# Attention with decay and a mixer on one core: idle matmuls placed by the planner's gaps, a score piece cut in two, wider low-part weights, another order

## The chip, the cores and the metric

The kernel runs on one core of one Trainium2 chip. The time is device time in microseconds (us) of one launch. Before the change it took 1146.36 us, the median of 3 runs (1143.42 to 1152.19). Where the text speaks of engines it uses the names of the profile: PE is the matrix engine, PEld its weight loads, DVE the vector engine, ACT the scalar engine, POOL the GpSimd engine, SP the queue that issues transfers.

## What is computed

All inputs are float32. There are 8 batches of 8 heads, with a sequence of 576 and a head size of 64, so 512 channels. First comes causal attention with a decay, then a mixer over tokens and channels:

```python
log_f = np.log(np.clip(f, 0.0001, 1.0)); cum = np.cumsum(log_f, axis=-1)
scores = scale * (q @ k.T) + cum[:, None] - cum[None, :]      # causal
attn = softmax(scores);  x = attn @ v                         # per head, then heads side by side
xt = x.transpose(0, 2, 1)
h = np.maximum(xt @ w_tok1, 0.0) @ w_tok2                     # 576 -> 256 -> 576
u = x + h.transpose(0, 2, 1)
out = u + np.maximum(u @ w_ch1, 0.0) @ w_ch2                  # 512 -> 1536 -> 512
```

## The kernel before

**Two parts.** The first part, some 690 us of the span, does the attention of all 64 heads, the token mixer, and the channel mixer for the first 256 of its 1536 hidden columns. The second part does the other 1280 hidden columns for nine blocks of 512 tokens: 2160 matmuls of 512 columns each, one behind the other (L819 to L842).

**High and low parts.** To keep float32 accuracy on a faster matmul type, an operand is split into a high part (its value rounded) and a low part (the rest). A product of two split operands is three matmuls: high by high, high by low, low by high.

**A head pair.** Two heads are loaded together (`raw`), q and k are split into `hl`, and their scores are computed by three score steps, `scores` (L504). The head size is 64, so a score matmul uses 64 of the 128 rows of the array; the two heads of a pair lie in the upper and lower half, and both halves work at the same time. A step computes some row blocks of head 0 and others of head 1. The row blocks (`where`, L494) have 64, 192, 320, 448 and 576 score columns; the one of 576 is computed as two pieces of 288. `PLACES` (L502) is the order of the pieces in a step: the first step has 288 and 288 in one half, 448 and 64 in the other; the second has 448 and 64 beside 320 and 192; the third 320 and 192 beside 288 and 288. Each list is gone through four times, for high by high, low by high, high by low, and the decay. A step is thus 16 matmuls (L519), each with a load of its own weights.

**The rest of a head.** DVE takes the masked row minimum (L560), ACT the exponential (L567), POOL divides by the row sum (L593), PE transposes the probabilities (L607), ACT and DVE split them, and PE multiplies them with the values into `av` (L677 to L689). The values lie as `vv`, 128 columns wide: 64 of the high part and 64 of the low part. The high part of the probabilities is multiplied with all 128 columns (L689); their low part with the first 64 alone (L687). ACT and DVE add the two halves of the result into `xt` (L727, L734, L737). The first four heads are done without the split.

**PSUM.** The first pair of banks (`pairs[0]`, kind `sc`) holds the 576-wide score blocks; the second (`pairs[1]`, kind `av`) the sums of `av`; four single banks hold all else (`one`).

**What sets the order.** Nothing is written in the order in which it runs. Each operation is given to a planner, `Plan.op`, with an engine, a duration, a priority and its buffers. `Plan.run` plays the program with these durations: on each engine the ready operation of the lowest priority number is taken next, if its buffers are free. The order in which operations start there is the order of the program, engine by engine; each engine then works through its own list, and waits where an operand isn't ready. The priorities are the table `PR`: one number for each operation of each head or mixer step, found by a search. A score step's duration in the plan is worked out from its columns (`flow`, L521).

**Idle matmuls.** `fill` (L346) gives the planner 120 small matmuls of the identity with itself, into an `av` buffer that nobody reads, with the worst priority there is, from a planned time of 8.5 us on. PE takes one wherever it has nothing else, until the 120 are used up.

Of the kernel before, what the change touches and what calls it, by code (L numbers as in the profile page):

```python
# [15 lines left out]
P = 128  # L16
PRM = dict(
    FILL=120, EP=3, DLAST=1, F1=2, FV=4, n_raw=2, n_vr=2, n_hl=2, n_vv=2,
# [5 lines left out]
    load=(-49.42, 46.29, 92.32, -145.75, 158.83, 224.67, 392.43, 389.92, 51.72, -48.13, -153.64, 61.83, 93.55, 627.95, -379.01, -179, 102.9, 208.23, 313.33, -46.54, 77.82, 682.62, 583.35, 565.73, 618.77, 476.42, 210.51, 132.03, -5.16, 471.13, 807.5, 123.55,),  # L24
    vload=(260.89, -123.21, -87.6, -152.37, -253.12, 178.61, -271.5, 143.23, -99.57, -242.66, 73.14, -320.19, -310.84, 74.82, 236.19, 70.39, -273.25, 388.84, -0.22, -78.47, -129.44, 469.63, 181.63, 387.34, 385.04, 230.17, 266.43, 60.11, 177.61, 138.15, -295.68, -169.11,),
    hi=(-129.17, -415.12, -86.61, 108.68, 306.45, -531.69, -232.24, 165.51, -110.63, -192.03, 59.44, 397.5, 237.73, -147.47, 14.26, -308.52, -51.97, -159.87, 7.58, 219.17, 246.51, -266.63, -191.79, 13.99, 118.63, -34.92, 136.84, 221.46, -3.49, 128.31, 0.66, -310.18,),
    lo=(-489.63, -34.98, 182.79, 104.62, -125.46, -287.97, -331.87, 31.39, 196.89, 23.66, -413.95, -451.42, 205.39, -749.32, -108.87, -107.11, 139.51, 29.45, -369.92, -169.78, -526.87, -68.1, 20.38, -250.48, -344.54, 32.69, 0.4, -425.79, -319.03, -206.8, 30.01, -364.65,),
    vh=(-31.37, -30.76, -94.41, -113.4, -515.02, -327.92, -378.35, -236.94, -123.95, -222.98, -393.91, -204.08, -65.62, -266.02, -57.45, -210.12, -445.93, -449.4, 241.14, -61.99, -170, -302.26, 92.7, -173.08, 59.29, 87.72, -184.46, 12.37, 222.89, 59.12, -54.28, -35.71,),
    vl=(560.64, 122.14, 152, 332.3, 65.87, -132.79, 356.3, -113.35, 230.75, 109.79, -25.3, 263.93, 170.51, 88.24, 216.55, -184.22, 82.02, 171.22, 163.44, 232.62, 254.57, -1.67, 94.46, -138.66, -53.34, -221.02, 284.67, 404.97, -273.49, -10.98, -61.7, -82.46,),
    s1=(125.56, 126.13, 107.5, 181.46, 251.3, -11.07, -68.97, -38.23, 111.08, -55.96, 102.57, 107.08, 620.08, 37.06, 38.4, 53.85, 56.06, -39.81, 90.27, 59.68, -34.99, 41.66, 60.32, 71.83, -4.82, 74.81, -75.81, 125.97, 101.21, 120.47, 95.31, 376.09,),  # L30
    s2=(-19.7, 325.83, -148.1, -274.85, -298.9, -96.51, -258.3, -199.59, 45.51, 1.37, -122.92, -387.8, 99.01, -173.56, -15.5, -267.47, -145.97, -162.18, 57.83, 246.58, 36.34, -417.88, 163.49, -11.16, -132.89, -15.37, -70.87, 132.08, -91.72, -104.46, -252.21, -23.22,),
    s3=(-106.81, -657.17, -171.91, -118.29, -371.64, -432.82, -87.4, -395.44, -313.1, -119.42, -181.81, -20.34, -248.25, -78.96, -171.97, -92.86, -158.9, -377.85, -86.62, -94.1, -200.53, -134.42, -176.82, 32.33, -174.48, -160.27, -110.2, -254.33, -277.72, -259.16, -31.29, -29.24,),
    mn4=(212.64, -151.19, 33.65, -60.63, 54.93, 214.65, 102.81, -42.6, -10.05, 258.69, 464.19, -23.01, 224.98, 253.21, 138.99, 85.09, -231.68, 137.58, 254.41, 84.48, 247.24, 35.75, 45.25, 101.38, -42.51, 181.55, 121.66, -140.73, -15.32, 23.02, 127.35, 86.04, 78.93, -65.2, 8.69, 352.28, 72.2, -73.1, 147.81, 158.41, -2.32, -23.53, -75.47, 58.34, 130.08, 187.04, 132.9, 77.49, 94.23, -51.57, 153.57, 25, -113.13, 30.6, 210.83, 114.09, 180.91, 164.75, 233.74, 327.77, 201.31, 361.67, 108.31, 100.26,),
    ex4=(192.92, 130.59, 156.67, -19.3, -289.51, 161.85, 302.86, -62.62, -65.42, 92.51, -3.84, -41.44, 59.97, -215.72, 87.59, 5.81, 203.67, 134.11, -135.58, 82.91, -215.04, 165.06, 405.95, 196.86, -28.28, 41.97, -65.17, 45.14, -70.21, 90.92, 108.74, -219.16, 255.08, 233.37, 17.69, 170.33, 289.37, 22.54, 199.44, 363.62, -174.81, -28.32, -100.02, -28.94, -283.21, 141.99, 88.75, 26.92, -70.16, 216.53, 107.37, 146.65, 244.62, -97.85, -46.68, 57.2, 202.95, 330.3, -50.94, -185.29, 39.67, 206.02, 374.73, 143.02,),
# [46 lines left out]
class Plan:  # L81
# [14 lines left out]
    def op(self, eng, dur, prio, fn, rd=(), wr=(), bufs=(), lat=0, at=0.0, port=False, span=None):  # L96
# [26 lines left out]
        for d in deps:  # L123
            d.outs.append(o)
        for b in bufs:
            b.left += 1
        self.ops.append(o)
        return o

    def run(self, slots):  # L130

        free = {k: None for k in slots}
        busy_unit = {}
        engines = {}
        for o in self.ops:
            engines.setdefault(o.eng, [])
# [43 lines left out]
        while left:  # L180
            moved = False
            for e, lst in ready.items():
# [71 lines left out]
def build(nc, env, dims):  # L254
# [97 lines left out]

    for i in range(PRM["FILL"]):
        fill(i)
# [862 lines left out]
```

## Time and profile before

| what | us |
|---|---|
| median of 3 runs | 1146.36 |
| lowest, highest | 1143.42, 1152.19 |
| the profiled execution, its time | 1153.54 |
| its span, from the first to the last instruction | 1151.7 |
| mean granted clock of PE | 0.987 |
| busy time in the span: PE, DVE, ACT, POOL | 1106.1, 630.6, 558.8, 526.0 |

The profiled execution took 7.2 us more than the median. A row of the profile names the line, the engine, the operation, the tile it writes and those it reads; "PE busy" counts matmuls from their start to a modelled end, and matmuls are pipelined, so that the distance between two starts says more than one duration. The granted clock is 1.00 at full speed.

### The profile page before, as it was taken

To read this page: it belongs to the slowest core of one execution; us is meant where nothing else is said; L and a number is where in the kernel's file an instruction comes from. 1 tells how busy PE (TensorE), PEld (TensorE's weight loads), DVE (VectorE), ACT (ScalarE), POOL (GpSimd) and SP (SyncE) were. 2 spreads that over 40 slices of the span, in tenths; PEclk is the share of its full clock that TensorE was granted. 3 is DMA by queue.
4 is the path that set the end of the run, shared out by engine and by line. 5 is a ranking of instruction groups with operands and counts; after the bars stand their busy time and mean duration, and the time that the engine had idled before them with its cause. 6 is when DMAs were issued, how large, how long until landed. Compare 5 with 4: busy or idle time off the path is not lost.

```text
span 1151.7 us, 19870 instructions
## 1 busy us (share of the span) xinstructions
PE 1106.1 (96%) x7310; PEld 955.8 (83%) x7310; DVE 630.6 (55%) x1622; ACT 558.8 (49%) x1441; POOL 526.0 (46%) x611
## 2 busy tenths in 40 slices
PE   8987786999999999999999999999999999999998
PEld 7676675998999899889999888888888888888886
DVE  7578787878767787787777996121212121212111
ACT  6577666767777787787786543121111111111110
POOL 2788676783848786786662403220303030312010
PEclk9999898999999999999999999999999999999999
DMA  5232222233212223222103543321203030302010
GB/s 183 64 97 66 81 75 95 95 112 112 86 52 90 103 65 116 86 86 84 35 22 119 199 153 125 101 71 40 83 27 110 1 110 1 110 1 73 18 56 37
DMA packets 47490, 93.20 MB, mean 81 GB/s; under 512 B 6688, under 2 KB 24096, under 8 KB 46368
## 3 DMA queue, kind: packets, MB, share of 16 engines
q1 hardware_dynamic: 47392, 91.93, 24.4%
q8 instruction: 57, 0.93, 0.3%
q14 instruction: 41, 0.34, 0.1%
HBM read 63.60 MB, written 28.31 MB: 80 GB/s over the span
## 4 chain that ended last, share of the span: by engine, by line
PE 85%; DVE 6%; ACT 4%; POOL 2%; issue 2%; DMA 0%; SPq 0%; DVEq 0%; ACTq 0%; POOLq 0%
PE bank L607 8%; PE bank L820 7%; PE bank L819 7%; PE bank L821 7%; PE pair L841 7%; PE pair L840 7%; PE pair L842 7%; PE bank L519 7%; PE pair L689 3%; PE pair L687 3%; PE pair L519 2%; PE pair L677 2%; PE bank L1032 1%; ACT pr L567 1%; PE bank L1004 1%
## 5 line engine op out<-in xcount | busy, mean ns | idle before, releaser
L301 POOL TENSOR_TENSOR ring<-xt,ring 128x512 fp32r<-128x512 f32 (+1 forms) x68 | 93.0, 1384 | 333.6 <-ACT ring L295 332.3
L307 DVE SCALAR_TENSOR_TENSOR hid<-bank,hid 128x512 fp32r<-128x512 f32 x90 | 62.2, 691 | 334.2 <-ACT hid L295 334.2
L295 ACT ACTIVATE hid<-bank 128x512 fp32r<-128x512 f32 x90 | 53.8, 598 | 344.1 <-PE bank L821 343.9
L593 POOL TENSOR_SCALAR pr<-pr,rec 128x576 f32<-128x576 f32 (+4 forms) x320 | 163.5, 532 | 12.2 <-DVE rec L586 7.1
L295 ACT ACTIVATE p<-bank 128x384 fp32r<-128x384 f32 (+2 forms) x300 | 130.8, 475 | 49.1 <-PE bank L607 46.7
L607 PE MATMUL bank<-ident,pr 128*128 128x128 f32 (+1 forms) x960 | 145.7, 285 | 7.4 <-ACT pr L567 2.5
L841 PE MATMUL pair<-hid,w2r 128*128 128x512 f32 x360 | 140.1, 389 | 0.0
L840 PE MATMUL pair<-hid,w2r 128*128 128x512 f32 x360 | 140.1, 389 | 0.0
L820 PE MATMUL bank<-ring,w1r 128*128 128x512 f32 x360 | 140.1, 389 | 0.0
L821 PE MATMUL bank<-ring,w1r 128*128 128x512 f32 x360 | 140.0, 389 | 0.0
L819 PE MATMUL bank<-ring,w1r 128*128 128x512 f32 x360 | 140.0, 389 | 0.0
L842 PE MATMUL pair<-hid,w2r 128*128 128x512 f32 x360 | 140.0, 389 | 0.0
L607 PEld LDWEIGHTS bank<-ident,pr 128*128 128x128 f32 (+1 forms) x960 | 111.0, 136 | 27.7 <-ACT pr L567 4.9
L304 DVE TENSOR_TENSOR p<-bank,p 128x384 fp32r<-128x384 f32 (+1 forms) x180 | 106.1, 595 | 46.4 <-ACT p L295 44.9
L567 ACT ACTIVATE pr<-bank,nmin 128x448 f32<-128x448 f32 (+3 forms) x256 | 117.9, 468 | 23.3 <-DVE nmin L560 21.0
L560 DVE CUSTOM_DVE_ANT_0 bank<-bank,mask 128x320 f32<-128x320 f32 (+3 forms) x256 | 105.9, 442 | 22.8 <-PE bank L519 20.2
L519 PE MATMUL bank<-hl 64*128 64x64 f32 (+3 forms) x768 | 103.7, 308 | 2.9 <-DVE hl L489 1.8
L519 PEld LDWEIGHTS bank<-hl 64*128 64x128 f32 x768 | 83.9, 185 | 12.3 <-issue 3.0
L819 PEld LDWEIGHTS bank<-ring,w1r 128*128 128x128 f32 x360 | 67.6, 188 | 14.1
L842 PEld LDWEIGHTS pair<-hid,w2r 128*128 128x128 f32 x360 | 67.6, 188 | 14.0
L821 PEld LDWEIGHTS bank<-ring,w1r 128*128 128x128 f32 x360 | 67.5, 188 | 14.0
L841 PEld LDWEIGHTS pair<-hid,w2r 128*128 128x128 f32 x360 | 67.6, 188 | 14.0
(123 smaller groups left out, 2611.3 us busy)
## 6 DMA issues: line engine op xcount, KB each, us to landing
raw<-in_qk SPq DMA_DIRECT2D x32, 576.0 KB, 3.7
vr<-in_v SPq DMA_DIRECT2D x32, 320.0 KB, 2.9
ud<-xt SPq DMA_DIRECT2D x8, 1152.0 KB, 4.8
pd<-part SPq DMA_DIRECT2D x32, 288.0 KB, 2.1
out_t<-part SPq DMA_DIRECT2D x36, 256.0 KB, 2.6
d_raw<-in_w_ch SPq DMA_DIRECT2D x12, 512.0 KB, 3.5
d_raw<-in_w_ch SPq DMA_DIRECT2D x40, 128.0 KB, 3.0
xt<-ud SPq DMA_DIRECT2D x2, 1024.0 KB, 5.4
```

The lines of the kernel that those rows point to most:

```text
L295: nc.scalar.activation(out, in_, func, scale=scale)
L304: nc.vector.tensor_tensor(out, in_, asf(hi), op=ALU.subtract)
L519: nc.tensor.matmul(at(bs[x])[:m, of : of + w], left, right, start=first, stop=(z == 3), skip_group_check=True)
L567: nc.scalar.activation(at(pr)[:m, poff[t] : poff[t] + w], at(mybanks[k])[:m, of : of + w], AF.Exp, bias=E["nmin"][sm][:m, t : t + 1], scal ...
L593: nc.gpsimd.tensor_scalar(x, x, r, 0.0, op0=ALU.mult, op1=ALU.add)
L607: nc.tensor.transpose(out, at(pr)[:, poff[i] + start[j] : poff[i] + end[j]], E["ident"])
L819: nc.tensor.matmul(q, wh[:, c, :], h_, start=(c == 0), stop=False)
L820: nc.tensor.matmul(q, wl[:, c, :], h_, start=False, stop=False)
L821: nc.tensor.matmul(q, wh[:, c, :], l_, start=False, stop=(c == NC - 1))
L840: nc.tensor.matmul(q, wh, h_, start=(i == i0), stop=False)
L841: nc.tensor.matmul(q, wl, h_, start=False, stop=False)
L842: nc.tensor.matmul(q, wh, l_, start=False, stop=(i == NF - 1))
```

## The change

Four things are changed.

1. The 120 idle matmuls are no operations of the plan any more. When the plan is done, `run` goes through PE's list: where the planned start of an operation lies more than 400 ns behind the planned end of the one before (from 8.5 us on, and before the first operation of the second part), it puts in one idle matmul for every 112 ns of what is left of the gap after 150 ns. They are the same 64x64 product, but into the first pair of banks. There are 295 of them, in 44 groups: 47 in the first seven groups, 194 in the next 23, up to about the twentieth head, and 54 in the last 14. In 22 groups the first one waits for ACT or DVE: for the last reader of the score block that lies in that pair.
2. The score piece of 448 columns becomes two of 224 (`where`, `PLACES`), in the first two of the three score steps; these have 20 matmuls now. In the plan a step's duration is a constant (`SPANS`).
3. The low part of the probabilities is multiplied with all 128 columns of `vv`, not with 64. (The product of both low parts is thus added too.)
4. The planner adds the weight load ahead of an operation in full, where PE has stood idle, and the table `PR` is another one.

```diff
@@ PRM, PR
-    FILL=120, EP=3, DLAST=1, F1=2, FV=4, n_raw=2, n_vr=2, n_hl=2, n_vv=2,
+    EP=3, DLAST=1, F1=2, FV=4, n_raw=2, n_vr=2, n_hl=2, n_vv=2,
...
-    dec=(261.24, 234.03, -24.46, -117.88, 95.57, 16.32, -323.96, 147.46, 519.87, 667.7, 406.35, 248.6, -223.23, 335.2, 62.47,),
+    dec=(261.34, 336.18, -183.68, -1335.72, 449.89, 121.06, -247.23, 1292.58, -192.72, -183.15, 398.74, 395.04, -323.94, 832.72, 1008.01,),
@@ Plan.run
-    def run(self, slots):
+    def run(self, slots, each=112.0, spare=150.0, least=400.0):
...
-                    o.start += max(0.0, o.head - tail - (t - engine_at[e]))
+                    o.start += o.head if t > engine_at[e] else max(0.0, o.head - tail)
...
-        return order
+        out, at, seen, fit = [], 8500.0, 0.0, True
+        for o in order:
+            if o.eng == "PE":
+                fit = fit and not any(b.kind == "acc" for b in o.bufs)
+                for _ in range(int((o.start - max(at, seen) - spare) / each) if fit and o.start - max(at, seen) > least else 0):
+                    out.append(None)
+                seen = o.start + o.dur
+            out.append(o)
+        return out
@@ build
-    def fill(i):
-        av = Buf("av")
-        p.op(
-            "PE", [tp_(64, 64)] * 2, 1e6 + i, lambda: nc.tensor.matmul(at(av)[:64, :64], E["ident"][:, :64], E["ident"][:, :64], start=True, stop=True),
-            rd=[("fill", i - 1)], wr=[("fill", i)], bufs=[av], at=8500.0,
-        )
-
-    for i in range(PRM["FILL"]):
-        fill(i)
...
-        3: (0, [(0, 0, end[3])]),
+        3: (0, [(0, 0, end[3] // 2), (end[3] // 2, end[3] // 2, end[3] // 2)]),
...
-    PLACES = (((0, 0, 0), (1, 0, 0), (0, 0, 1), (1, 1, 0)), ((0, 0, 0), (1, 0, 0), (1, 1, 0), (0, 1, 0)), ((0, 0, 0), (1, 0, 0), (1, 0, 1), (0, 1, 0)))
+    PLACES = (
+        ((0, 0, 0), (1, 0, 0), (0, 0, 1), (1, 0, 1), (1, 1, 0)),
+        ((0, 0, 0), (1, 0, 0), (0, 0, 1), (1, 1, 0), (0, 1, 0)),
+        ((0, 0, 0), (1, 0, 0), (1, 0, 1), (0, 1, 0)),
+    )
+    SPANS = (1130, 1130, 1160)
...
-                        first = z == 0 and (x, u, s) != (0, 1, 0) and (x, u, s) != (1, 1, 0)
+                        first = z == 0 and u == 0 and (s == 0 or t == 4)
...
-            flow = [sum(where[t][1][s][2] + 30 for x, u, s in places if x == y for t in [units[x][u]]) for y in (0, 1)]
...
-                bufs=[*bs, hl, cc, *prs], span=4 * max(flow) / 2.4,
+                bufs=[*bs, hl, cc, *prs], span=SPANS[st],
...
-                elif z:
-                    nc.tensor.matmul(x[:D], at(vv)[:, v0 + j, :D], at(pb)[:, 1, c0 : c0 + w], start=False, stop=last)
                 else:
-                    nc.tensor.matmul(x, at(vv)[:, v0 + j, :], at(pb)[:, 0, c0 : c0 + w], start=False, stop=last)
+                    nc.tensor.matmul(x, at(vv)[:, v0 + j, :], at(pb)[:, z, c0 : c0 + w], start=False, stop=last)
...
-            return [tp_(w, D)] * 2 if fv else [mm_(w, D if z else P)]
+            return [tp_(w, D)] * 2 if fv else [mm_(w)]
@@ attn_mixer_kernel
-            o.fn()
+            if o is None:
+                nc.tensor.matmul(pairs[0][:64, :64], ident[:, :64], ident[:, :64], start=True, stop=True)
+            else:
+                o.fn()
```

**The idle matmuls, on PE.** The place is the seam between a score step and the product of the next head with its values, some ten heads into the kernel; pair_63 is the first pair of banks, pair_64 the second, hl the split q and k, p the split probabilities, cc and sel the decay. In the kernel before:

```order
L519 MATMUL bank_66<-cc_181,sel 128x448
L519 MATMUL bank_68<-cc_181,sel 128x320
L519 MATMUL bank_68<-cc_181,sel 128x192
L519 MATMUL bank_66<-cc_181,sel 128x64
L677 MATMUL pair_64<-p_179,vv_169 128x512 [waits DVE_49,Pool_49]
L678 MATMUL pair_64<-p_179,vv_169 128x64
```

and in the changed one:

```order
L525 MATMUL bank_65<-cc_181,sel 128x224
L525 MATMUL pair_63<-cc_181,sel 128x288
L525 MATMUL bank_65<-cc_181,sel 128x224
L525 MATMUL bank_65<-cc_181,sel 128x64
L1186 MATMUL pair_63<-ident 64x64 [waits DVE_49]
L1186 MATMUL pair_63<-ident 64x64 x6
L682 MATMUL pair_64<-p_179,vv_169 128x512 [waits Activation_49,Pool_49]
```

Seven idle matmuls now stand between the two; the first waits for DVE, and the product behind it can't start before they are done.

**The score step, on PE.** The place is the first score step of a head pair; the pair of banks takes the pieces of one half of the array, the single bank those of the other. Before, the first round of the list and half of the second:

```order
L519 MATMUL pair_63<-hl_167 128x288
L519 MATMUL bank_68<-hl_167 128x448 [waits DVE_49]
L519 MATMUL pair_63<-hl_167 128x288
L519 MATMUL bank_68<-hl_167 128x64
L519 MATMUL pair_63<-hl_167 128x288
L519 MATMUL bank_68<-hl_167 128x448
```

and now:

```order
L525 MATMUL pair_63<-hl_167 128x288
L525 MATMUL bank_65<-hl_167 128x224 [waits DVE_49]
L525 MATMUL pair_63<-hl_167 128x288
L525 MATMUL bank_65<-hl_167 128x224
L525 MATMUL bank_65<-hl_167 128x64
L525 MATMUL pair_63<-hl_167 128x288
L525 MATMUL bank_65<-hl_167 128x224
```

The half that had two matmuls in a round has three.

**The low-part products, on PE.** The place is the end of a head's product with its values; L607 and L612 are transposes. Before:

```order
L687 MATMUL pair_64<-p_178,vv_169 64x512
L689 MATMUL pair_64<-p_178,vv_169 128x512
L607 MATMUL bank_68<-ident,pr_170 64x128 [waits Activation_49]
L607 MATMUL bank_68<-ident,pr_170 64x128 x3
L687 MATMUL pair_64<-p_177,vv_169 64x384
L689 MATMUL pair_64<-p_177,vv_169 128x384
L607 MATMUL bank_66<-ident,pr_170 128x128 [waits Activation_49]
L607 MATMUL bank_66<-ident,pr_170 128x128 x3
L689 MATMUL pair_64<-p_175,vv_169 128x128
L687 MATMUL pair_64<-p_175,vv_169 64x128
L687 MATMUL pair_64<-p_175,vv_169 64x256
L689 MATMUL pair_64<-p_175,vv_169 128x256
```

and now:

```order
L692 MATMUL pair_64<-p_178,vv_169 128x512 x2
L612 MATMUL bank_68<-ident,pr_170 128x128 x4
L692 MATMUL pair_64<-p_177,vv_169 128x384 x2
L692 MATMUL pair_64<-p_175,vv_169 128x128 x2
L692 MATMUL pair_64<-p_175,vv_169 128x256 x2
L1186 MATMUL pair_63<-ident 64x64 [waits Activation_49]
```

The matmuls with 64 output rows (64 weight columns) have become such of 128.

More of the change, by code (lines that the diff above doesn't have):

```diff
@@ L55 @@
-    dec=(261.24, 234.03, -24.46, -117.88, 95.57, 16.32, -323.96, 147.46, 519.87, 667.7, 406.35, 248.6, -223.23, 335.2, 62.47,),
-    dec3=(255, 25.19, 499.74, 240.41, 567.3, -35.26, 303.23, 374.53, 943.87, 473.14, 15.68, 538.77, 239.12, 427.46, 113.5, 413.03, 54.45, 726.31, -291.68, 188.64,),
+    load=(-26.73, 348.68, -358.7, 122.05, 324.23, -0.33, -122.99, -24.62, 685.99, 667.1, -479.32, 410.03, 81.06, 337.64, 196.53, 75.93, 383.27, 363.51, 785.72, 522.6, 273.36, 765.15, -6.37, 1052.06, 476.09, -84.99, -167.06, -288.69, 379.79, 594.27, -287.98, 943.95,),
@@ new lines @@
+    vload=(845.68, -924.72, -1126.55, -934.92, -352, 355.5, -404.65, -341.25, 303.04, 68.76, -556.5, 477.26, 10.88, 665.03, 279.55, 206.64, 237.9, 379.23, 332.57, -13.11, -752.27, -631.35, -163.64, -127.64, 344.58, -417.03, -191.73, 74.37, 728.52, 427.92, -370.46, -413.02,),
+    hi=(-114.51, -153.5, -196.61, 102.29, -496.82, -102.33, -545.96, -70.78, -459.5, 316.23, -30.58, -212.26, -353.33, -167.74, -656.64, 46.01, 161.55, -73.1, 59.29, -34.72, -506.16, 28.52, 319.79, 357.98, -260.28, -722.21, 406.89, 73.5, -232.67, -306.36, 381.71, -1068.88,),
@@ new lines @@
+    lo=(-310.59, -165.92, 143.75, -613.39, -463.53, -621.67, 344.22, -457.84, 196.98, 23.57, 209.18, 34.15, -37.41, -569.78, 24.91, -209.74, 207.72, 212.77, -122.22, 436.03, -245.07, 186.67, -671.59, -705.05, 375.29, 70.63, 165.6, -755.32, -106.92, -37.55, -23.2, -140.82,),
+    vh=(-129.29, -210.57, -122.35, -207.5, 181.64, -124.39, -100.97, -425.53, -230.48, -683.14, -401.82, -1.06, 239.27, -183.92, -377.6, 205.6, 54.62, 90.64, -280.74, -448.12, 765.03, -316.2, -163.34, -11.69, -85.27, -684.47, -96.37, -62.66, -259.85, 366.19, -246.6, 409.46,),
@@ new lines @@
+    vl=(-167.12, -70.45, 299.09, 122.7, 267.82, 156.47, -333.23, 20.1, 916.32, 558.9, 137.92, -225.84, 595.83, -212.99, -158.6, 462.91, 0.29, -318.43, -335.07, 1261.47, 541.79, -244.27, 672.57, 103.15, 304.68, 107.86, -133.22, -158.2, -377.77, 20.53, -621.72, -663.56,),
+    s1=(-185.93, -55.69, -459.38, -70.2, 430.22, 179.86, -49.96, -641.16, 908.39, 172.58, 801.82, 73.51, -411.44, 232.48, 89.49, 12.42, -267.97, -344.02, 57.95, 64.32, -208.48, 51.72, 183.62, -502.18, 22.81, -4.61, 219.91, 106.66, 79.65, 301.44, 157.94, -51.65,),
@@ new lines @@
+    s2=(-211.54, 111.53, -125.77, -118.05, 73.33, 335.78, 284.27, 277.34, 34.01, -404.44, 13.27, 207.9, 540.14, -626.43, -140.97, -58.83, -284.99, -653.89, 173.47, -584, -22.16, -488.23, -254.24, 418.22, -88.46, -76.01, 50.87, 43.05, -95.76, -175.64, 142.56, -148.81,),
+    s3=(-1315.91, -346.52, 313.26, -117.06, -251.98, -482.32, -283.9, -189.53, -362.78, -743.44, -317.25, -216.57, -468.72, -187.28, -536.36, -449.6, -105.27, -288.64, -324.14, -689.66, -195.22, -347.34, -518.32, -334.72, -250.63, -413.8, 55.74, -255.91, -194.33, 13.98, -389.93, -601.06,),
```

54 lines of the change are left out of this document (23 added, 31 removed).

## The prediction

> **What bounds the kernel now.** I read the page first, then the busy time by stage (the window view, cut where PE changes its habits), then the half-speed windows of PE, then the chain.
>
> ```profile
> span 1151.7 us, 19870 instructions
> PE 1106.1 (96%) x7310; PEld 955.8 (83%) x7310; DVE 630.6 (55%) x1622; ACT 558.8 (49%) x1441; POOL 526.0 (46%) x611
> ...
> 0.00:75.00 75.00, 70.21 (x638) 51.47 (x639) 51.00 (x169) 48.73 (x141) 43.62 (x67) 1.00 0.38 120
> 75.00:200.00 125.00, 95.86 (x736) 82.84 (x735) 96.32 (x272) 83.58 (x236) 91.18 (x113) 0.89 0.23 75
> 200.00:690.00 490.00, 483.49 (x3919) 443.46 (x3919) 390.28 (x1043) 353.87 (x944) 304.47 (x364) 1.00 0.28 95
> 690.00:1152.00 462.00, 456.55 (x2022) 378.06 (x2020) 92.99 (x142) 72.57 (x125) 86.71 (x68) 1.00 0.19 61
> ```
>
> The columns are the busy times of PE, its weight loads, DVE, ACT and POOL, then PE's granted clock, DMA share and GB/s. PE is the bound from 200 us on: 6.5 us idle in 490, and the last stage, which the change leaves alone, is a closed row of matmuls. Between 75 and 200 us nothing is full: PE is idle for 125 - 95.86 = 29.1 us, yet its clock is 0.89. Cut to 3.41 us, that stretch has these windows at half speed, all there are before 1140 us (the first row is a full-speed one):
>
> ```profile
> 126.04:129.45 3.41, 1.80 (x16) 1.49 (x14) 3.39 (x15) 2.66 (x9) 0.12 (x1) 1.00 0.00 0
> 81.66:85.08 3.42, 3.32 (x13) 2.77 (x14) 1.84 (x8) 2.42 (x9) 3.42 (x5) 0.50 0.35 85
> 112.38:115.80 3.42, 3.42 (x16) 2.88 (x15) 2.09 (x6) 2.48 (x9) 3.42 (x5) 0.50 0.27 73
> 119.21:122.62 3.41, 2.90 (x12) 2.53 (x13) 1.10 (x4) 0.84 (x3) 2.00 (x2) 0.50 0.10 14
> 129.45:132.86 3.41, 3.41 (x16) 2.85 (x15) 2.67 (x8) 2.98 (x11) 0.80 (x1) 0.50 0.30 84
> 146.52:149.93 3.41, 3.41 (x17) 3.14 (x16) 2.21 (x5) 2.28 (x7) 1.31 (x2) 0.50 0.00 0
> 173.83:177.24 3.41, 0.65 (x3) 0.58 (x4) 2.55 (x6) 1.18 (x3) 2.40 (x3) 0.50 0.34 70
> 177.24:180.65 3.41, 3.41 (x17) 2.96 (x16) 1.36 (x3) 1.18 (x3) 2.04 (x5) 0.50 0.25 103
> 184.07:187.48 3.41, 3.41 (x14) 2.84 (x15) 1.28 (x4) 1.18 (x3) 1.36 (x2) 0.50 0.32 96
> ```
>
> The window ahead of 129.45 had PE busy 1.80 of 3.41 us, about half, and half speed followed; so it is ahead of the others. When PE then gets its work, it does it at half speed: 16 matmuls fill a window. The chain of waits shows what that does:
>
> ```profile
> 75.20 0.88 PE bank L607 x8
> ...
> 82.58 1.76 PE bank L607 x8
> ...
> 116.08 2.85 POOL pr L593 x6
> ...
> 120.57 1.76 PE bank L607 x8
> ...
> 184.66 1.76 PE bank L607 x8
> ```
>
> The same eight transposes take 0.88 us at full speed and 1.76 at half, and they lie on the chain. At 112 to 119 us POOL is the chain, and at 173.83 PE had next to nothing to do.
>
> **The change part by part.** The sum is made against the profiled execution: 1153.54 us, a span of 1151.7 and 1.8 around it, which is 7.2 above the median of 1146.36.
>
> *Idle matmuls.* Until 75 us the old ones stand and the clock is 1.00 throughout; behind them it falls. The new ones stand in the gaps that follow (194 of them up to about the twentieth head), so the half-speed windows should go. Worth at most half of PE's busy time in the eight: 3.32 + 3.42 + 2.90 + 3.41 + 3.41 + 0.65 + 3.41 + 3.41 = 23.9, half of it 12.0 us. Without the two windows where PE is not the chain it is 19.9, half of it 9.9. DVE, at 96 of 125 us, is late next, so I take -8, between -3 and -12. The idle matmuls themselves lie in idle time, 29.1 us of it. What they add is a wait: PE works in order, and in 22 groups the first one waits until DVE and ACT have read the 576-wide score block; behind it stand transposes and products of other heads, for which in turn ACT and DVE wait. The two reads that may be outstanding:
>
> ```profile
> L560 DVE CUSTOM_DVE_ANT_0 pair<-pair,mask 128x576 f32<-128x576 f32 x64 | 49.9, 779 | 5.9 <-PE bank L519 5.8
> L567 ACT ACTIVATE pr<-pair,nmin 128x576 f32<-128x576 f32 x64 | 47.4, 740 | 28.8 <-DVE nmin L560 27.5 <-PE bank L519 1.2
> ```
>
> So a wait costs from nothing to 0.78 + 0.74 = 1.5 us. Most groups stand in planned gaps of the stretch where PE waits anyway; I take +1 in all, with 22 x 1.5 = 33 as the far end.
>
> *Score halves.* One first step, PE and then its loads:
>
> ```profile
> 420.80 0.29 PE L961 MATMUL bank<-t2h,ring 128*128 128x288 f32 x1
> 421.01 0.40 PE L519 MATMUL pair<-hl 64*128 64x288 f32 x1
> ...
> 421.67 0.44 PE L519 MATMUL bank<-hl 64*128 64x448 f32 x1
> 421.78 0.29 PE L519 MATMUL pair<-hl 64*128 64x288 f32 x1
> 421.91 0.30 PE L519 MATMUL pair<-cc,sel 64*128 64x288 f32 x1
> 421.95 0.19 PE L519 MATMUL bank<-hl 64*128 64x64 f32 x1
> ...
> 422.26 0.19 PE L519 MATMUL bank<-cc,sel 64*128 64x64 f32 x1
> 422.38 0.55 PE L607 MATMUL bank<-ident,pr 128*128 128x128 f32 x3
> ```
>
> ```profile
> 421.33 0.18 PEld L519 LDWEIGHTS bank<-hl 64*128 64x128 f32 x1
> ...
> 421.44 0.19 PEld L519 LDWEIGHTS bank<-hl 64*128 64x128 f32 x1
> ```
>
> The step takes 422.38 - 421.01 = 1.37 us. The half with 288 and 288 goes at 0.13 a piece, 0.26 a round; the half with 448 and 64 needs 422.26 - 421.95 = 0.31 a round and sets the step. Two loads for the same half, one straight after the other, start 0.11 apart. A short matmul can't hide that: the 64-column piece costs a load, 0.11, and 448 columns 0.20. At the pace of the 288 piece 224 columns take 0.13 x 224 / 288 = 0.10, less than a load. So a round becomes three loads, 0.33 us, and a step 4 x 0.02 = 0.08 longer. The same pieces are in the second step. The window view of two lines alone says how many there are in the dense stage:
>
> ```profile
> 200.00:690.00 490.00, 88.64 (x1024) 76.16 (x1024) 1.00 0.28 95
> ...
> 200.00:690.00 490.00, 54.40 (x184) 21.55 (x184) 1.00 0.28 95
> ```
>
> The first row is L519: 1024 / 16 = 64 steps in the stage that PE bounds, two thirds of them changed, 43 x 0.08 = +3.4; with some of the 12 before 200 us, +4. The other end: if loads didn't bind, the 0.26 of the other half would set the round, 43 x 4 x 0.05 = -8.6.
>
> *Low-part products.* The second row above is L687: 184 / 4 = 46 heads there. The end of one such product, and its loads:
>
> ```profile
> 418.89 0.31 PE L689 MATMUL pair<-p,vv 128*128 128x128 f32 x1
> 419.04 0.34 PE L687 MATMUL pair<-p,vv 128*64 128x128 f32 x2
> 419.22 0.28 PE L689 MATMUL pair<-p,vv 128*128 128x256 f32 x1
> 419.34 0.29 PE L959 MATMUL bank<-t2h,ring 128*128 128x288 f32 x1
> ```
>
> ```profile
> 418.98 0.20 PEld L687 LDWEIGHTS pair<-p,vv 128*64 128x64 f32 x2
> 419.10 0.19 PEld L689 LDWEIGHTS pair<-p,vv 128*128 128x128 f32 x1
> ```
>
> Two loads of 64 columns take 0.12 together, 0.06 each, half of the 0.11 above; so the two 128-column matmuls, which are short enough to be bound by the load behind them, take 0.06 each now and 0.11 with 128-column weights: +0.10 a head. The products of 256 to 512 columns hide either load. 46 x 0.10 = +4.6, and +5 with a little of the 13 earlier heads; as much as +7 where the short first product (L678) is followed by such a load, and about 0 if all were hidden.
>
> The Trainium skill says otherwise (TensorEngine Tiling (Array Packing), Key Properties): changing the tiling mode drains TensorE, and 128x64 is another mode than 128x128. By that rule leaving the 64-column form saves drains; that is the fourth rival below. The trace shows a drain where the rows change (above, 420.80 to 421.01, 0.21 instead of the 0.13 of its kind, so 0.08) but none at the columns, where 0.06 is the load alone.
>
> *The new order.* It moves every engine's list and the transfers (the DMA share of 0.23 to 0.28 leaves these room). What it can win is idle PE: 4.8 + 29.1 + 6.5 = 40 us before 690 us. In the dense stage a searched order left 6.5 of 490; the 29 are where there is something to find. I take -8, a quarter of these, between +4 and -25.
>
> Sum: -8 + 1 + 4 + 5 - 8 = -6, so 1147.5 for an execution like the profiled one. Of the 7.2 us by which that one lies above the median I put half down to its half-speed windows, which need not fall alike in each run, and which the forecast has already taken out; the other half comes off: 1144.
>
> **The rivals.** *The order pays more* (faster): half of the 40 us of idle time, 20 rather than 8. For it: the stretch to 200 us is bound by no engine. Against: the same waits on DVE and POOL stand in any order. 1144 - 12 = 1132. (A score round of 0.26 would come to the same, 1144 - 4 - 8.6 = 1131.)
>
> *The idle matmuls block PE* (slower): the waits of the 22 groups for the score block's readers come late in fact, since the planned times aren't the real ones. At 0.7 us each they cost 15 us and push the time over 1% up; at 1 us, 1144 + 21 = 1165. For it: the reads take 1.5 us. Against: 16 of the 22 stand before about 200 us, where PE has 29 us to spare.
>
> *The clock isn't kept* (the change doesn't do what it says): real gaps aren't where the plan has them, half-speed windows remain, 1144 + 8 = 1152. Against: the old ones kept it until 75 us.
>
> *Column modes drain*: six changes a head (two at each of three places) at the 0.08 of the row change, 46 heads, give -22, and the +5 falls away: 1144 - 27 = 1117. Against: the loads above.
>
> **How the numbers follow.** A measurement of this kernel can tell about 1% from no change: below 1134.9 is faster, above 1157.8 slower. The forecast, 1144 within 1%, gets 0.58; the clock not kept, which also ends within 1%, 0.10; the order paying more 0.21; column modes 0.03; blocked PE 0.08. So faster 0.24, same 0.68, slower 0.08. The range goes from 1129, which takes in most of the second case, to 1157; outside it lie the column modes, the blocked PE and a good third of the better order, 0.03 + 0.08 + 0.08.
>
> **What would show it.** Clock: no half-speed windows between 75 and 200 us, and the eight transposes at 0.88 us everywhere. Scores: 1.45 us for the first step, loads of the half with three pieces 0.11 apart. Low parts: in the last group of a head 0.22 us, not 0.12, from the first load of a low part to the load behind the second. Idle matmuls: hardly any wait of theirs for ACT or DVE in the list of waits. Order: PE's idle time before 690 us falls from 40 by about 8, beyond what the clock gives. If PE's idle time grows or the clock stays at 0.89, the prediction is wrong in its first step; if the score step falls below 1.37, in its second.

## The result, and the profile after

| | before | after |
|---|---|---|
| first comparison, medians in us (4 runs each) | 1146.62 | 1159.27 (1157.69 to 1159.59) |
| its ratio, 95% interval | | 1.0102 [1.0062, 1.0143] |
| repeated beside the experiments (19 and 10 runs) | 1151.69 | 1157.77 (1156.94 to 1159.54) |
| its ratio, 95% interval | | 1.0058 [1.0040, 1.0077] |
| the profiled execution, its span | 1153.54, 1151.7 | 1159.12, 1157.3 |

The change makes the kernel slower, by 0.4 to 1.4%; the forecast was 1144, in a range that ends at 1157. The kernel before had medians of 1151.4 to 1151.9 in each of the later sessions, so 1.0058 is the better figure, some 7 us. Prices below are differences of ratios to the runs of before beside them, times 1151.5 us.

First the page of the changed kernel and its busy time by stage (PE, its loads, DVE, ACT, POOL; granted clock, DMA share, GB/s):

```profile
span 1157.3 us, 21062 instructions
PE 1135.2 (98%) x7916; PEld 994.4 (86%) x7916; DVE 622.9 (54%) x1622; ACT 560.8 (48%) x1441; POOL 527.4 (46%) x611
...
PE 94%; DVE 3%; ACT 2%; issue 1%; DMA 0%; SPq 0%; DVEq 0%; ACTq 0%
```

```profile
0.00:75.00 75.00, 68.90 (x583) 51.31 (x584) 52.33 (x176) 49.80 (x142) 44.63 (x68) 0.95 0.38 118
75.00:200.00 125.00, 116.38 (x1155) 104.50 (x1154) 93.40 (x274) 85.28 (x240) 93.39 (x115) 0.97 0.27 84
200.00:690.00 490.00, 487.60 (x4139) 455.79 (x4138) 378.47 (x1023) 350.43 (x931) 302.52 (x362) 1.00 0.28 92
```

PE is busier, 98% instead of 96%, it makes up 94% of the chain that ended last (the third line; 85% before), and its clock from 75 to 200 us is 0.97 instead of 0.89. Read alone, these lines say that the change worked. But the same stages for the idle matmuls alone:

```profile
0.00:75.00 75.00, 11.11 (x136) 0.95 0.38 118
75.00:200.00 125.00, 26.38 (x350) 0.97 0.27 84
200.00:690.00 490.00, 9.27 (x108) 1.00 0.28 92
```

That is 46.75 us of PE's busy time before 690 us (each idle matmul leaves two records). PE's true idle time there is 6.10 + 8.62 + 2.40 = 17.1 us, so 64 us hold no work of the problem; before the change it was 40 us and the 120 old idle matmuls. The list of PE's waits begins with the idle ones:

```profile
PE pair L1186 <- ACT pr L572: 6.0, 5, 3.3
PE pair L1186 <- DVE nmin L565: 4.1, 5, 1.1
```

So for 10.1 us PE stands in front of an idle matmul that waits for the readers of the score block (microseconds, times, the longest). The longest is this one, and below it the read that it waits for:

```profile
175.41 5.46 PE L1186 MATMUL pair<-ident 128*64 128x64 f32 x60 [3.31 <-ACT pr L572]
```

```profile
174.54 0.73 ACT L572 ACTIVATE pr<-pair,nmin 128x576 f32<-128x576 f32 x1
```

ACT comes to that read only at 174.54, since other work stands ahead of it in ACT's own list; PE has stood since 172.1. Of the windows at half speed, four are left, two of them where before had none:

```profile
12.03:15.44 3.41, 3.23 (x29) 3.10 (x28) 2.96 (x15) 2.71 (x7) 1.53 (x2) 0.50 0.56 186
15.45:18.86 3.41, 3.41 (x33) 3.29 (x32) 1.85 (x5) 1.10 (x5) 0.00 (x0) 0.50 0.15 29
172.46:175.87 3.41, 0.46 (x4) 0.46 (x5) 2.08 (x6) 2.85 (x9) 1.61 (x3) 0.50 0.55 173
175.88:179.29 3.41, 3.41 (x35) 3.41 (x34) 0.00 (x0) 0.00 (x0) 3.41 (x7) 0.50 0.00 0
```

One first score step, from its first product to the transposes behind it:

```profile
438.32 0.40 PE L525 MATMUL pair<-hl 64*128 64x288 f32 x1
...
439.78 0.44 PE L612 MATMUL bank<-ident,pr 128*128 128x128 f32 x2
```

It takes 1.46 us (1.37 before). The loads of the products with the values, behind the first group:

```profile
424.04 0.53 PEld L692 LDWEIGHTS pair<-p,vv 128*128 128x128 f32 x4
```

Four loads in 0.53 us, the last of them 0.19 by itself as before: they start (0.53 - 0.19) / 3 = 0.11 apart, also those of the low parts, which were 0.06 apart.

### The profile page after: what moved, and what is told of

Read it like the earlier page. It is cut to its first block, busy times and chain, and to the rows that moved or that the text cites. A ratio compares the mean times of both kernels' runs of the same rounds, so it can differ in the third digit from the quotient of the medians.

```text
span 1157.3 us, 21062 instructions
## 1 busy us (share of the span) xinstructions
PE 1135.2 (98%) x7916; PEld 994.4 (86%) x7916; DVE 622.9 (54%) x1622; ACT 560.8 (48%) x1441; POOL 527.4 (46%) x611
## 4 chain that ended last, share of the span: by engine, by line
PE 94%; DVE 3%; ACT 2%; issue 1%; DMA 0%; SPq 0%; DVEq 0%; ACTq 0%
PE bank L612 9%; PE bank L525 8%; PE bank L824 7%; PE bank L823 7%; PE bank L822 7%; PE pair L845 7%; PE pair L844 7%; PE pair L843 7%; PE pair L692 6%; PE pair L1186 3%; PE pair L525 3%; PE bank L938 2%; PE pair L682 2%; PE bank L962 2%; PE bank L1035 2%; PE bank L1007 2%
## 5 line engine op out<-in xcount | busy, mean ns | idle before, releaser
L598 POOL TENSOR_SCALAR pr<-pr,rec 128x576 f32<-128x576 f32 (+4 forms) x320 | 164.3, 534 | 23.3 <-DVE rec L591 17.1
L303 ACT ACTIVATE p<-bank 128x384 fp32r<-128x384 f32 (+3 forms) x300 | 129.8, 474 | 49.5 <-PE bank L612 44.7
L612 PE MATMUL bank<-ident,pr 128*128 128x128 f32 (+1 forms) x960 | 138.9, 275 | 1.8 <-DVE p L312 1.3
L565 DVE CUSTOM_DVE_ANT_0 bank<-bank,mask 128x448 f32<-128x448 f32 (+3 forms) x256 | 106.3, 441 | 28.7 <-PE bank L525 27.0
L612 PEld LDWEIGHTS bank<-ident,pr 128*128 128x128 f32 (+1 forms) x960 | 106.5, 131 | 16.6 <-DVE p L312 1.7
L525 PE MATMUL bank<-hl 64*128 64x224 f32 (+3 forms) x960 | 109.6, 287 | 2.7 <-DVE hl L490 1.8
L692 PE MATMUL pair<-p,vv 128*128 128x512 f32 x480 | 109.4, 342 | 0.0
L525 PEld LDWEIGHTS bank<-hl 64*128 64x128 f32 x960 | 96.4, 189 | 11.7 <-issue 2.5
L823 PEld LDWEIGHTS bank<-ring,w1r 128*128 128x128 f32 x360 | 67.6, 188 | 14.1
## 6 DMA issues: line engine op xcount, KB each, us to landing
ud<-xt SPq DMA_DIRECT2D x8, 1152.0 KB, 4.6
```

What stands on the lines that cost most here:

```text
L303: nc.scalar.activation(out, in_, func, scale=scale)
L525: nc.tensor.matmul(at(bs[x])[:m, of : of + w], left, right, start=first, stop=(z == 3), skip_group_check=True)
L598: nc.gpsimd.tensor_scalar(x, x, r, 0.0, op0=ALU.mult, op1=ALU.add)
L612: nc.tensor.transpose(out, at(pr)[:, poff[i] + start[j] : poff[i] + end[j]], E["ident"])
L692: nc.tensor.matmul(x, at(vv)[:, v0 + j, :], at(pb)[:, z, c0 : c0 + w], start=False, stop=last)
L823: nc.tensor.matmul(q, wl[:, c, :], h_, start=False, stop=False)
```

## The experiments

**Each part alone.** Three kernels put one part of the change into the kernel before; a fourth keeps the new order alone. The cuts of code are shortened, with `...` where lines are left out.

Low-part products on 128 columns:

```diff
-                elif z:
-                    nc.tensor.matmul(x[:D], at(vv)[:, v0 + j, :D], at(pb)[:, 1, c0 : c0 + w], start=False, stop=last)
                 else:
-                    nc.tensor.matmul(x, at(vv)[:, v0 + j, :], at(pb)[:, 0, c0 : c0 + w], start=False, stop=last)
+                    nc.tensor.matmul(x, at(vv)[:, v0 + j, :], at(pb)[:, z, c0 : c0 + w], start=False, stop=last)
```

> The kernel before with one part of the change alone: the low-part products on 128 columns, order and everything else as before. My theory (a weight load of 128 columns costs 0.05 us more than one of 64, and nothing hides it behind a 128-column product): +0.10 us a head on PE, 46 to 59 heads, so +5 us (between +3 and +7), ratio 1.003 to 1.006. Rival (changing the column mode drains PE, and the wide form saves six drains a head): a gain of up to 20 us, ratio 0.98 to 0.99. Rival (the planner's other durations, not the loads, make the cost): no difference.

Measured: 1155.99, ratio 1.0048 [1.0029, 1.0067], +5.5 us. That is the forecast by loads. The Trainium skill (TensorEngine Tiling (Array Packing), Key Properties) has a change of tiling mode drain TensorE; by that the wide form should have gained, and here it lost what the loads cost, so at 64 against 128 weight columns no drain shows.

The score piece in halves, with the plan's durations kept so that the order stays:

```diff
-        3: (0, [(0, 0, end[3])]),
+        3: (0, [(0, 0, end[3] // 2), (end[3] // 2, end[3] // 2, end[3] // 2)]),
...
+    SPANS = (4 * 636 / 2.4, 4 * 572 / 2.4, 4 * 636 / 2.4)
...
```

> The kernel before with the score piece of 448 columns in two halves alone, order as before. My theory (three short matmuls in one half of the array are bound by their loads, 0.11 us each): the first and second score step 0.08 to 0.09 us longer each; 43 to 55 steps lie where PE is the bound: +3.5 to +5 us, ratio 1.003 to 1.004. Rival (the step's end isn't what others wait for, since PE takes other work meanwhile): no difference, though the step is longer. Rival (the other half of the array sets the round): the step 0.2 us shorter and 8 us less.

Measured: 1153.38, ratio 1.0011 [0.9988, 1.0033]: between -1.4 and +3.8 us. The first step is 0.09 us longer (1.46 us in this run too), as expected, and the forecast of +3.5 is inside the interval, but so is nothing at all. The third case, a step that is 0.2 us shorter, falls.

Idle matmuls in the planned gaps of the order before, 364 beside its own 120:

```diff
+            if o is None:
+                nc.tensor.matmul(pairs[0][:64, :64], ident[:, :64], ident[:, :64], start=True, stop=True)
```

> The kernel before with idle matmuls in the planned gaps alone (its own 120 kept, some 340 more from the planned gaps of its own order, into the first pair of banks, as the change does it). First theory, that of the prediction (they keep the clock, and lie in idle time): no half-speed windows between 75 and 200 us, and 3 to 10 us less, ratio 0.991 to 0.997. Rival (they stand in PE's in-order list in front of real work and wait for the readers of the score block): the clock is kept as well, but idle matmuls wait, and the time is the same or up to 10 us more. Rival (the clock did not cost anything, because PE was waited for by nobody there): clock kept, time the same within 2 us, hardly any waits of idle matmuls.

Measured: 1166.57, ratio 1.0126 [1.0101, 1.0150], +14.5 us, though the clock was kept: 0.995 to 0.999 in the executions of this kernel, 0.986 to 0.992 in those of the kernel before beside them. What the prediction's first two terms make -7 together, clock and waits, comes out as +14.5 here.

The new order without idle matmuls, with the whole piece and the narrow low parts. It is the changed kernel, its plan with the same durations and priorities, and this is undone in what it issues:

```diff
-        3: (0, [(0, 0, end[3] // 2), (end[3] // 2, end[3] // 2, end[3] // 2)]),
+        3: (0, [(0, 0, end[3])]),
...
+                elif z:
+                    nc.tensor.matmul(x[:D], at(vv)[:, v0 + j, :D], at(pb)[:, 1, c0 : c0 + w], start=False, stop=last)
...
-            if o is None:
-                nc.tensor.matmul(pairs[0][:64, :64], ident[:, :64], ident[:, :64], start=True, stop=True)
-            else:
+            if o is not None:
```

> The changed kernel's order alone, without idle matmuls, with the 448-column piece whole and 64-column low parts. Prediction's theory (the order is worth 8 us, between a gain of 25 and a loss of 4): with a clock no better than the kernel before's, 1139 to 1150 us. Rival (the order was found for a plan that counts the halves, the wide low parts and the idle matmuls, and is no better in itself): the same as before or up to 10 us more, with half-speed windows at least as many as before, also in the first 75 us, since no idle matmul is left at all. What this run and the three others add up to, against the 12.7 us that the whole change costs, tells whether the parts act alone.

Measured: 1133.41, ratio 0.9836 [0.9809, 0.9864], -18.9 us, with a mean clock of 0.984, below the 0.987 of before. Its stages:

```profile
0.00:75.00 75.00, 64.14 (x427) 43.24 (x428) 55.72 (x182) 53.31 (x154) 48.26 (x72) 0.92 0.40 127
75.00:200.00 125.00, 111.04 (x863) 95.80 (x862) 103.99 (x304) 92.16 (x262) 97.72 (x118) 0.91 0.28 88
200.00:690.00 490.00, 484.37 (x3855) 443.51 (x3852) 383.77 (x1020) 348.99 (x921) 297.94 (x358) 1.00 0.28 94
```

By 200 us DVE has done 486 instructions where it had done 441, ACT 416 where it had done 377. The gain is made early. The rows below are the products that open the ninth and the seventeenth head, first in the kernel before, then in the new order (count, least, median and longest ns, first and last start):

```profile
L677 PE MATMUL pair<-p,vv x1: 393/393/393, 98.3 to 98.3; 128*128 128x512 f32 x1
...
L677 PE MATMUL pair<-p,vv x1: 657/657/657, 183.9 to 183.9; 128*128 128x512 f32 x1
```

```profile
L678 PE MATMUL pair<-p,vv x1: 474/474/474, 98.1 to 98.1; 128*128 128x512 f32 x1
...
L678 PE MATMUL pair<-p,vv x1: 765/765/765, 165.6 to 165.6; 128*128 128x512 f32 x1
```

The ninth starts at the same time, the seventeenth 18.3 us sooner. This is the fastest kernel of the study, ahead of the kernel before and of the changed one. It has no idle matmuls at all, so part of the gain is the 120 old ones that are gone: against the kernel before without these (0.9979, below) the order itself is worth 0.9979 - 0.9836, 16.5 us.

**The changed kernel without idle matmuls.**

```diff
-            if o is None:
-                nc.tensor.matmul(pairs[0][:64, :64], ident[:, :64], ident[:, :64], start=True, stop=True)
-            else:
+            if o is not None:
                 o.fn()
```

> The changed kernel without any idle matmul; halves, wide low parts and order stay. If the parts add up (order alone 0.984 of before, wide low parts 1.005, halves 1.001): 0.989 to 0.990 of before, about 1138 to 1141 us, so that the idle matmuls alone cost the changed kernel some 19 us. Rival (the new order is only good without the halves and the wide low parts): 1150 us or more.

Measured: 1139.46, ratio 0.9905 [0.9880, 0.9930]. The parts add up: order, wide low parts and halves would give 0.9836 + 0.0048 + 0.0011 = 0.9895. And the idle matmuls alone, with all that they bring, cost 1.0058 - 0.9905, 17.6 us.

**Waits or work.** These kernels keep some of the 295 idle matmuls of the changed kernel. `g` is the place, `m` the number within it; the condition is all that differs. `free`, `waiting` and `early` stand for lists of places that are written out in the kernels. There are 43 places (the two groups at the kernel's start count as one): in 22 the first idle matmul waits for ACT or DVE, in 21 for neither.

One in each place:

```diff
+                if m == 0:
```

> The changed kernel with one idle matmul in each place instead of up to 30: 43 rather than 295. Every wait that the first one of a place brings is kept, the work is down to 43 x 0.12 = 5 us. Theory A (the waits cost: PE stands behind a reader of the score block while other work is ready): near the changed kernel, 1152 to 1160 us. Theory B (the work costs: 36 us of idle matmuls in gaps that are not there on the chip or stand elsewhere): 1140 to 1146 us, a little above the kernel with none.

Measured: 1151.81, ratio 1.0004 [0.9978, 1.0029]: 11.4 us above the kernel without any, at a seventh of the idle work.

Only places where the first one waits for no reader (19 of the 21, the kernel's start among them; the other two hold 26 idle matmuls):

```diff
+                if g in free:
```

> The changed kernel with idle matmuls only in the 20 places where the first one waits for no reader of a score block: 110 of the 295. Theory A (waits cost): as the kernel with none, 1138 to 1142 us, or 3 to 6 us better if the clock gains by them. Theory B (the work costs): 110 x 0.12 = 13 us of work, of which half or more shows: 1145 to 1153 us.

Measured: 1142.36, ratio 0.9924 [0.9904, 0.9944]: +2.2 us for 110 idle matmuls.

One in each of the 22 waiting places, and one in each of the two places that the kernel above leaves out:

```diff
+                if m == 0 and g not in free:
```

> The changed kernel with a single idle matmul in each of the 22 places where it waits for a reader of a score block, and none elsewhere: the waits without the work (22 x 0.12 = 2.6 us). Theory A (waits cost): nearly all of the loss, 1150 to 1158 us. Theory B (work costs): 1138 to 1143 us, as the kernel with none. In between, the loss is shared in that proportion.

Measured: 1153.47, ratio 1.0016 [0.9994, 1.0038]: +12.8 us for 24 idle matmuls (48 records, two each; the expectation counts 22), 0.53 us each. The first two of them in this kernel, and below it the second place in the kernel without any:

```profile
15.31 0.47 PE L1190 MATMUL pair<-ident 128*64 128x64 f32 x2
15.71 0.61 PE L525 MATMUL pair<-hl 64*128 64x288 f32 x1
...
17.65 0.82 PE L525 MATMUL bank<-cc,sel 64*128 64x224 f32 x3
19.57 0.48 PE L1190 MATMUL pair<-ident 128*64 128x64 f32 x2 [1.09 <-DVE nmin L565]
19.98 0.79 PE L525 MATMUL bank<-hl 64*128 64x224 f32 x4
```

```profile
17.67 0.49 PE L525 MATMUL bank<-cc,sel 64*128 64x224 f32 x2
18.22 1.84 PE L525 MATMUL bank<-hl 64*128 64x320 f32 x13
```

The next score step writes another bank; in the kernel without any it starts at 18.22. Here it starts at 19.98, since PE takes its list in order: 1.09 us until DVE has read the score block, and 0.41 us for the idle matmul itself, from 19.57 to 19.98. The one at 15.31 cost 0.40 in the same way, though PE did not stand in front of it. The first product that opens a head comes out 2.8 us late:

```profile
L682 PE MATMUL pair<-part,vr x1: 640/640/640, 28.5 to 28.5; 64*64 64x512 f32 x1
```

```profile
L682 PE MATMUL pair<-part,vr x2: 589/614/640, 31.3 to 31.8; 64*64 64x512 f32 x2
```

The whole kernel's waits in front of idle matmuls are:

```profile
PE pair L1190 <- ACT pr L572: 5.3, 3, 3.3
PE pair L1190 <- DVE nmin L565: 3.6, 4, 1.4
...
PE pair L1190 <- ACT ring L303: 0.7, 1, 0.7
...
PE pair L1190 <- ACT part L618: 0.5, 1, 0.5
```

That is 10.1 us, but it isn't 10.1 us more than before: in return PE stands less in front of the products that open a head. Here, and below it in the kernel without any:

```profile
PE pair L682 <- DVE xt L737: 2.0, 2, 1.3
```

```profile
PE pair L682 <- DVE xt L737: 6.0, 3, 2.6
```

Over the whole span PE is idle for 34.8 us here and for 31.8 without any, so 3.0 us more, and busy for 6.9 us more: with the idle matmuls, and with the same work at a lower clock (0.979 against 0.982 in these two executions). That the waiting places make the loss is shown; how it divides between standing, the idle matmuls and the clock is not.

The 16 waiting places before about 200 us, one in each, and not the six later ones:

```diff
+                if m == 0 and g in early:
```

> The changed kernel with one idle matmul in each of the 16 waiting places that stand before about 200 us, none in the six later ones and none elsewhere. The prediction's argument (a wait there lies in PE's idle time and is free; the dear ones are the six later ones): 1139 to 1143 us. My theory (PE's idle time there is no slack, the chain goes through DVE, ACT and PE in turn, and each wait is added to it): 1149 to 1154 us, 10 us or more above the kernel without idle matmuls. 22 waits cost 14 us, 0.64 us each; shared evenly, 16 would cost 10 us: 1149.5.

Measured: 1151.59, ratio 1.0001 [0.9981, 1.0020]: +11.1 us, nearly the whole price. So the waits are dear just where PE has idle time.

All 159 idle matmuls of the 22 waiting places, and the changed kernel once more beside it:

```diff
+                if g in waiting:
```

> The changed kernel with all the idle matmuls of the 22 waiting places (159) and none of the 110 in places that don't wait; the other 26 are left out too. One in each of these places cost 1.1% of before (1.0016 against 0.9905). Theory A (the first one's wait is all; those behind it fill a gap that is there): as with one each, 0.999 to 1.004. Theory B (what stands behind a wait that ended late lies on the chain too, so their work shows: 137 more at 0.12 us are 16 us, at least a third of it 5): 1.006 to 1.015, about the changed kernel itself.

> The changed kernel once more, on the same chip as the run above. By its parts (order 0.984, wide low parts 1.005, halves 1.001, idle matmuls 1.020): 1.009 to 1.013 of before, and 0.000 to 0.008 above the kernel with only the waiting places.

Measured: 1157.92, ratio 1.0057 [1.0037, 1.0077], and 1157.77, ratio 1.0058 [1.0040, 1.0077]. The waiting places alone make as large a loss as all 295. Their 137 further matmuls, some 16 us of work, add 1.0057 - 1.0016, 4.7 us. That is between both theories' figures, with intervals that just touch, so about three quarters of the loss come with the first idle matmul of a place, and the rest, less surely, with those behind it.

**What a kept clock is worth.** Three kernels keep or lose it without any waits of idle matmuls. Each changes the idle work together with the clock, so it prices the two in one.

The new order with the 110 free ones (the condition of the free places, in the kernel of the order alone):

```diff
-            if o is not None:
+            if o is None:
+                if g in free:
+                    nc.tensor.matmul(pairs[0][:64, :64], ident[:, :64], ident[:, :64], start=True, stop=True)
+            else:
                 o.fn()
```

> The new order without halves and wide low parts, with idle matmuls only in the 20 places where they wait for no reader: 110 of them. Theory 1 (the clock is worth time once nothing waits): 1127 to 1131 us, 0.979 to 0.982 of before, below the order alone (0.984). Theory 2 (full speed only makes PE wait longer for the others, and the work shows a little, as the 2.9 us that the same 110 added to the changed kernel): 1134 to 1138 us, 0.985 to 0.988.

Measured: 1135.50, ratio 0.9873 [0.9840, 0.9905], at a mean clock of 0.990 instead of 0.984. It is 2.1 us above the order alone by medians and 4.3 by ratios, with intervals that overlap; it gains nothing.

The kernel before without its own 120:

```diff
-            "PE", [tp_(64, 64)] * 2, 1e6 + i, lambda: nc.tensor.matmul(at(av)[:64, :64], E["ident"][:, :64], E["ident"][:, :64], start=True, stop=True),
+            "PE", [tp_(64, 64)] * 2, 1e6 + i, lambda: None,
```

> The kernel before in its order, its own 120 idle matmuls left out. Theory 1 (they keep the clock in the first 75 us, and that is worth time): half-speed windows there, 3 to 8 us slower, 1.003 to 1.007. Theory 2 (their work stands in front of real work, and the first head's product, which starts 4.9 us later than in the new order, is late for it): the same or up to 5 us faster, 0.996 to 1.000.

Measured: 1147.73, ratio 0.9979 [0.9952, 1.0007]: between 5.5 us faster and 0.8 slower, and so not slower by what a lost clock was to cost. Its first stages:

```profile
0.00:75.00 75.00, 60.92 (x397) 42.43 (x397) 50.91 (x169) 48.18 (x141) 43.45 (x67) 0.86 0.37 120
75.00:200.00 125.00, 99.11 (x793) 86.92 (x793) 98.09 (x285) 88.01 (x245) 95.98 (x117) 0.93 0.26 83
200.00:690.00 490.00, 483.50 (x3897) 442.80 (x3897) 390.47 (x1043) 352.44 (x938) 301.17 (x360) 1.00 0.28 95
```

At a clock of 0.86 DVE, ACT and POOL have done 169, 141 and 67 instructions by 75 us: the very counts that the kernel before reached at 1.00. But that kernel also has 120 idle matmuls in PE's list. And a delay is there before 75 us: the products that open the first four heads, in the kernel before and then in this one, start 0.9 us later.

```profile
L677 PE MATMUL pair<-part,vr x8: 589/614/640, 31.8 to 55.7; 64*64 64x512 f32 x8
```

```profile
L677 PE MATMUL pair<-part,vr x8: 589/614/640, 32.7 to 56.6; 64*64 64x512 f32 x8
```

The Trainium skill (TensorE: Matmul & The Clock Gate, Terms) puts the penalty at the throttled time times the share of pulses left out. By that rule the clock of 0.86 over 75 us would cost 10.5 us, an estimate; the kernel as a whole isn't slower, net of the idle work that it is rid of. By the same rule 0.001 of mean clock over a span of 1152 us would be 1.15 us, an estimate too; the executions of one program, below, show 0.5 to 1.3.

The kernel before with 158 more, in those planned gaps where they wait for no reader:

> The kernel before in its order with idle matmuls in those planned gaps where they wait for no reader: 158 more, in 15 places, beside its own 120. The prediction's first term by itself, without its waits. Theory 1 (a kept clock is worth 3 to 12 us): 0.990 to 0.997 of before. Theory 2 (it is worth nothing that the 158 x 0.12 = 19 us of work doesn't take back): 0.998 to 1.005.

Measured: 1151.46, ratio 0.9998 [0.9975, 1.0021], though the clock is up:

```profile
75.00:200.00 125.00, 106.43 (x977) 94.83 (x976) 96.22 (x279) 85.57 (x240) 94.25 (x115) 0.95 0.26 83
```

0.95 instead of 0.89, and no time won by the median. Against the 1.0126 of the kernel with all 364, it also shows that in the order before the loss lies in the 16 places that wait, with the other 206.

**One program at two clocks.** None of these kernels changes the clock alone, but the executions of one program do: the mean clock differs from one to the next, and the time with it.

| executions of one program | at the lowest clock, us | at the highest clock, us |
|---|---|---|
| the kernel before, 95 in four sessions | 0.986: 1155.2 to 1156.0 | 0.994 and 0.995: 1143.4 to 1147.9 |
| the changed kernel, 10 in one session | 0.993: 1159.4 to 1159.5 | 0.998: 1156.9 to 1157.0 |

A line through each session gives 1.0 to 1.3 us for 0.001 of clock in the kernel before, 0.9 in the changed kernel without idle matmuls and 0.5 in the changed kernel. Two profiled executions of the changed kernel show which comes first. The one at 0.993, then the one at 0.998:

```profile
11.94 1.62 PE L525 MATMUL bank<-hl 64*128 64x224 f32 x13
...
14.67 2.61 PE L1186 MATMUL pair<-ident 128*64 128x64 f32 x22 [0.18 <-ACT pr L572]
17.21 0.61 PE L525 MATMUL pair<-hl 64*128 64x288 f32 x1
```

```profile
11.96 0.96 PE L525 MATMUL bank<-hl 64*128 64x224 f32 x13
...
14.68 1.50 PE L1186 MATMUL pair<-ident 128*64 128x64 f32 x22 [1.29 <-ACT pr L572]
16.11 0.40 PE L525 MATMUL pair<-hl 64*128 64x288 f32 x1
...
0.00:75.00 75.00, 68.22 (x601) 49.96 (x602) 53.79 (x178) 51.66 (x149) 45.77 (x70) 1.00 0.38 120
```

The score steps up to here start within 0.02 us of each other. Then the first execution has its half-speed windows (12.03 to 18.86, above), and the same idle matmuls take 2.61 us instead of 1.50, so that the score step behind them starts 1.1 us later. By 75 us ACT has done 142 instructions at the lower clock and 149 at the higher, and the whole span is 2.1 us longer (1157.3 and 1155.2). So the clock has a price here.

It stays hidden in the three kernels above because idle work has one as well. At equal clock, 0.988, the kernel with the 110 free ones took 1142.5 and that without any 1138.8 to 1139.1. At 0.993 the changed kernel took 1159.4 to 1159.5, that with the waiting places alone 1155.1 to 1155.8; the kernel before with 158 more 1150.5 to 1152.0, that without them 1147.8 and 1148.1. By these few executions, 110 to 158 idle matmuls that wait for nothing cost some 4 us, and the clock that they keep gives about as much back. That is an estimate; no run changed the clock alone.

## Why the prediction was wrong

| term of the sum | forecast, us | measured alone, us |
|---|---|---|
| idle matmuls keep the clock | -8 | not alone |
| their waits in PE's queue | +1 | +17.6, with their work, and net of the clock |
| score halves | +4 | +1.3 (-1.4 to +3.8) |
| low parts on 128 columns | +5 | +5.5 (3.3 to 7.7) |
| new order | -8 | -18.9 (-22 to -16), with the old 120 gone |
| sum | -6 | +5.5; the whole change +6.7 |

**The waits.** The step that failed is "Most groups stand in planned gaps of the stretch where PE waits anyway; I take +1 in all", and with it the idle work, put at nothing because the idle matmuls "lie in idle time". In their place the runs show +17.6 us for the 295, three quarters of it with the first one of each waiting place. The mechanism was there as a rival, with its 22 groups, its two readers and a price from which it decides (0.7 us each, 15 us), and it got 8 in 100. What stood against it, that 16 of the 22 lie where PE has 29 us to spare, is the mistake: one idle matmul in each of the 16 alone costs 11.1 us. The price of a wait was capped too low as well: 1.5 us counts the two reads themselves, and the longest wait took 3.3, since the reader had to come first in its own list. PE's idle time there is no store from which others may draw. PE is idle there because the chain goes through PE, DVE and ACT in turn, and what holds PE up when a step becomes ready is added to the chain, as between 17 and 31 us above.

**The clock.** It came back nearly as forecast: where before had eight windows at half speed, two are left, and two came up at 12 us, where the old idle matmuls are gone. The size, -8, can't be checked alone. By the executions of one program it isn't far off: from 0.987 without idle matmuls (0.988 in the kernel before) to 0.996 with them, by medians, at 0.5 to 0.9 us for 0.001, would be 5 to 8 us, an estimate. The waits and the work would then have cost 23 to 26 us, and the +17.6 is what is left of that. So the gain was there or nearly so, and was lost by what it takes to keep the clock: even where idle matmuls wait for nothing, three kernels show no net gain.

**The order.** The mechanism was right and the size off: -18.9 instead of -8, the size of the rival with half of the idle time. The room was taken as the 40 us that PE is idle before 690 us. The 120 old idle matmuls count as busy there; without them PE is idle for 14.1 + 25.9 + 6.5 = 46.5 us, and in the new order alone for 10.9 + 14.0 + 5.6 = 30.5. So 16 us of idle time went, where 8 were taken, and the order against the same kernel without idle matmuls is worth 16.5.

**Low parts and halves.** Both came from the distance of two loads, and the durations came out as forecast: 0.11 us between the loads, 1.46 us for the step (1.45 forecast). For the low parts the time agrees as well; for the halves it can't be told from nothing.

**The offset.** Taking off 3.6 us because the profiled execution lay above the median was wrong too: 1153.54 was no outlier, but near the 1151.5 that the kernel before takes in the other sessions. Counted from there the sum of the forecast gives 1145.5, still too low by 12. That half-speed windows needn't fall alike in each execution was right: the clock of the kernel before ran from 0.986 to 0.995.

**The rivals.** They were treated as cases of which one would hold. Two of opposite sign held together, the better order with -19 and the blocked PE with +18, and their difference is a small change that shows neither. The column modes that drain are out, by the wide low parts.

## What to carry to other kernels

An idle instruction is not free because its engine is idle on average: ask what it must wait for and what stands behind it in an in-order list, and put it only where it waits for nothing. A kept clock has a price, and so has the work that keeps it: weigh the two together, and read the worth of the clock from executions of one program that differ in it, not from kernels that differ in work too. And when several edits come together, run each alone: this change holds a version that is 1.6% faster than before, hidden under an edit that costs nearly as much.

## What the runs showed of the hardware

An idle matmul of 64 columns between two score steps held PE for 0.40 us (15.31 to 15.71 and 19.57 to 19.98, both in windows at half speed). In a row they follow one another after 0.21 us at half speed and 0.12 at full speed: (2.61 - 0.37) / 21 and (1.50 - 0.22) / 21 for one record in the 22 above, two records each.

The granted clock of one and the same program differed between executions, from 0.986 to 0.995 in the kernel before, and its time with it, from 1156.0 to 1143.4 us. The medians of that kernel lay between 1146.4 and 1151.9 us in the sessions of this study, 0.5% apart; only comparisons with runs beside them carry the smaller effects here.
